# Eight tiny loads between two bulk loads of a DMA-bound decode kernel

## The chip, the cores and the metric

The kernel runs on one core of a Trainium2 chip. The metric is the time of one execution on the device, in microseconds (us). "Before" is the kernel without the change.

## The reference

One decode step of a transformer block: attention over a cached K and V, then a small dense block. Nearly all the bytes are the two caches.

```python
B, Sq, D = 4, 1, 640
H, Sk, Dh = 32, 4096, 128          # k_cache, v_cache: (B, H, Sk, Dh) bf16, 134 MB each
q = layernorm(x) @ wq              # one query per head
p = softmax(q . k_cache * Dh**-0.5)
h = x + (p . v_cache) @ wo
out = h + mish(layernorm(h) @ w1 + b1) @ w2     # b1 has 1728 elements
```

## The kernel before

The caches are cut into 16 tiles (four groups of eight heads, four batches). K and V of a tile are 8 MB each (128 partitions of 64 KB) and are loaded whole into one of three slots of SBUF, A, B and C. SP issues all these loads on its own DMA queue, each as soon as its slot is free. DVE multiplies K by the query in place, PE folds the products, DVE and ACT make the exponentials, PE multiplies them by V.

```python
def load(p, dst, src, key, sem):            # every DMA goes through this line
    p.do(lambda: p.eng.dma_start(out=dst, in_=src), key, sem, 16)

KS = {0: "A", 1: "B", 2: "A", 3: "B"}       # slot of K of tile i, by i % 4
VS = {0: "C", 1: "C", 2: "A", 3: "C"}       # slot of V

def sync_prog():                            # SP's program; need() waits
    for hg in range(NHG):                   # head groups 0..3, i = 4 * hg
        ...
        sp.need(("F", i + 1, NS - 1))       # K of tile i + 1 used up
        k_load(i + 3)
        sp.need(("F", i + 2, NS - 1))
        v_load(i + 2)
        sp.need(("PV", i + 1))              # V of tile i + 1 used up
        v_load(i + 3)
    sp.need(("F", NT - 1, NS - 1))
    for q in range(NHG):
        load(sp, wo_sb[:, q, :, :], ...)    # output weights, then w1, w2
    ...
```

The softmax here doesn't subtract the row's maximum and nothing guards it: scores larger than these inputs give would overflow.

## Time and profile before

| | before |
|---|---|
| time, median of 2 runs | 664.68 us (664.61 to 664.76) |
| span of the profiled execution | 662.8 us |
| PE busy, DVE busy | 60%, 61% |
| mean DMA rate | 428 GB/s |

These lines come from the page of before. The row "DMA" gives the busy share of the 16 DMA engines in tenths for 40 equal slices of the span, "GB/s" what they moved in each, and the line "q1" is SP's queue: packets, megabytes, and the time of its packets as a share of 16 engines' span.

```profile
PE 396.2 (60%) x2747; PEld 79.9 (12%) x1787; DVE 406.8 (61%) x252; ACT 41.5 (6%) x158; POOL 2.6 (0%) x14
DMA  9999999999999999999999999999999999999996
GB/s 381 440 435 415 424 440 439 437 439 436 412 439 439 435 431 439 439 427 427 443 431 435 435 443 431 423 439 428 435 439 443 431 423 439 431 431 439 425 414 275
q1 hardware_dynamic: 6208, 283.27, 98.9%
HBM read 283.35 MB, written 0.01 MB: 428 GB/s over the span
```

No compute engine is near full, and the DMA engines have work in every slice but the last. The kernel is bound by its stream of loads.

The place that the change touches is the middle of the third head group (i = 8). This is SP's timeline of before there: start in us, length in us, engine and line, what was issued.

```profile
403.98 0.33 SPq L249 DMA_DIRECT2D slotB<-in_A_k_cache_dram  x1
436.73 0.33 SPq L249 DMA_DIRECT2D slotA<-in_A_v_cache_dram  x1
437.10 0.43 SPq L249 DMA_DIRECT2D slotC<-in_A_v_cache_dram  x1
467.79 0.33 SPq L249 DMA_DIRECT2D slotA<-in_A_k_cache_dram  x1
```

They are K of tile 11, V of tile 10, V of tile 11 (in short V11), and K of tile 12. When V10 and V11 were issued, K11 was still being moved. The trace also holds one record for every DMA packet (time, length, bytes, queue, but not the DMA engine). From them: nearly every 64 KB packet (98% of them) takes 2418 ns, an engine has eight per load, and each engine ends one 8 MB load 19.319 us after the one before, from about the tenth load to the last with hardly an exception. That is 8.389 MB / 19.319 us = 434 GB/s. The Trainium skill ("DMA: Bandwidth & Descriptors", "Where 436 GB/s comes from") gives 435.2 GB/s as the ceiling of the ways into SBUF; this trace comes within 0.3% of it.

The 16 engines are not in step. The first ends a load 2.0 us ahead of the last, and each keeps its distance from load to load. An engine that runs ahead of the last one has a **lead**. A load has landed only when the last engine has ended it.

The chain of waits that ended last, in order of time (start, length, what), begins at 616.7 us, and its long piece is the landing of the output weights:

```profile
625.33 22.87 DMA slotB<-in_A_wo_dram
648.20 0.05 issue
648.25 1.77 PE y_ps L706 x40
```

These weights are queued behind all the K and V loads.

### The profile page before, as it was taken

To read this page: it belongs to the slowest core of one execution; us is meant where nothing else is said; L and a number is where in the kernel's file an instruction comes from. 1 tells how busy PE (TensorE), PEld (TensorE's weight loads), DVE (VectorE), ACT (ScalarE), POOL (GpSimd) and SP (SyncE) were. 2 spreads that over 40 slices of the span, in tenths; PEclk is the share of its full clock that TensorE was granted. 3 is DMA by queue.
4 is the path that set the end of the run, shared out by engine and by line. 5 is a ranking of instruction groups with operands and counts; after the bars stand their busy time and mean duration, and the time that the engine had idled before them with its cause. 6 is when DMAs were issued, how large, how long until landed. Compare 5 with 4: busy or idle time off the path is not lost. (4 is left out here: it accounts for less than half of the span.)

```text
span 662.8 us, 5202 instructions
## 1 busy us (share of the span) xinstructions
PE 396.2 (60%) x2747; PEld 79.9 (12%) x1787; DVE 406.8 (61%) x252; ACT 41.5 (6%) x158; POOL 2.6 (0%) x14
## 2 busy tenths in 40 slices
PE   0847667657317595738417485848535656765866
PEld 0600010101101010101100010010110001010246
DVE  1067988486049678767218798848306798848612
ACT  0210000000000000000000000000000000000011
POOL 1000000000000000000000000000000000000000
PEclk9768797979759697958767887787866879797975
DMA  9999999999999999999999999999999999999996
GB/s 381 440 435 415 424 440 439 437 439 436 412 439 439 435 431 439 439 427 427 443 431 435 435 443 431 423 439 428 435 439 443 431 423 439 431 431 439 425 414 275
DMA packets 6546, 283.50 MB, mean 428 GB/s; under 512 B 964, under 2 KB 1032, under 8 KB 1544
## 3 DMA queue, kind: packets, MB, share of 16 engines
q1 hardware_dynamic: 6208, 283.27, 98.9%
q8 instruction: 7, 0.11, 0.1%
q10 hardware_dynamic: 328, 0.09, 0.1%
q14 instruction: 3, 0.02, 0.0%
HBM read 283.35 MB, written 0.01 MB: 428 GB/s over the span
## 5 line engine op out<-in xcount | busy, mean ns | idle before, releaser
L513 DVE TENSOR_TENSOR slotA<-slotA,q_bc 128x8192 bf16<-128x8192 bf16 x32 | 140.6, 4415 | 106.9 <-DMA slotA<-in_A_k_cache_dram 106.9
L513 DVE TENSOR_TENSOR slotB<-slotB,q_bc 128x8192 bf16<-128x8192 bf16 x32 | 140.7, 4416 | 14.8 <-DMA slotB<-in_A_k_cache_dram 14.8
L524 DVE TENSOR_REDUCE s_f<-red 128x64 f32<-128x1024 f32 x64 | 78.0, 1218 | 99.1 <-PE red L716 99.1
L716 PE MATMUL red<-slotA,ident 128*128 128x512 bf16 x480 | 138.2, 452 | 0.0
L716 PE MATMUL red<-slotB,ident 128*128 128x512 bf16 x480 | 126.8, 424 | 0.0
L706 PE MATMUL red<-slotA,ident 128*128 128x512 bf16 x32 | 14.3, 448 | 120.0 <-PEq L49 120.0
L706 PE MATMUL pv<-slotC,e 128*32 128x512 bf16 x768 | 52.0, 430 | 38.3 <-PEq L49 35.3
L706 PE MATMUL red<-slotB,ident 128*128 128x512 bf16 x32 | 14.1, 440 | 85.5 <-PEq L49 85.5
L392 ACT ACTIVATE ex<-s_f 128x64 bf16<-128x64 f32 x64 | 16.4, 256 | 503.5 <-DVE s_f L524 503.5
L538 DVE TENSOR_TENSOR e<-ex,hmask 128x512 bf16<-128x512 bf16 x64 | 39.8, 682 | 0.0
L706 PEld LDWEIGHTS pv<-slotC,e 128*32 128x32 bf16 x768 | 22.2, 107 | 96.3 <-issue 82.4
L706 PEld LDWEIGHTS red<-slotA,ident 128*128 128x128 bf16 x32 | 3.2, 99 | 189.0 <-issue 188.9
L706 PEld LDWEIGHTS red<-slotB,ident 128*128 128x128 bf16 x32 | 3.2, 99 | 168.7 <-issue 168.7
L706 PEld LDWEIGHTS o_ps<-pv_sb,selo 128*32 128x32 f32 x136 | 13.5, 109 | 64.0 <-issue 64.0
L706 PE MATMUL o_ps<-pv_sb,selo 128*32 128x128 f32 x136 | 18.0, 276 | 0.0
L706 PE MATMUL pv<-slotA,e 128*32 128x512 bf16 x256 | 14.5, 380 | 0.5 <-PEq L49 0.4
L402 ACT COPY pv_sb<-pv 128x512 f32<-128x512 f32 x16 | 9.4, 585 | 70.4 <-PE pv L706 70.4
L392 ACT ACTIVATION_READ_ACCUMULATOR ex<-s_f 128x1 f32 x64 | 11.9, 186 | 0.0
L706 PE MATMUL red<-q_all,sel 32*128 32x128 bf16 x128 | 10.0, 268 | 0.8 <-PEq L49 0.8
L706 PEld LDWEIGHTS red<-q_all,sel 32*128 32x128 bf16 x128 | 9.7, 121 | 1.7 <-issue 1.7
L706 PEld LDWEIGHTS pv<-slotA,e 128*32 128x32 bf16 x256 | 6.9, 97 | 23.5 <-issue 17.8
L706 PE MATMUL red<-slotC,lnT 128*32 128x512 bf16 x40 | 4.5, 630 | 8.8 <-PEq L49 8.8
(96 smaller groups left out, 73.7 us busy)
## 6 DMA issues: line engine op xcount, KB each, us to landing
slotC<-in_A_v_cache_dram SPq DMA_DIRECT2D x2, 4096.0 KB, 40.1
slotC<-in_A_wq_dram SPq DMA_DIRECT2D x1, 5120.0 KB, 16.1
slotB<-in_A_wo_dram SPq DMA_DIRECT2D x4, 1280.0 KB, 19.0
slotB<-in_B_w_dram SPq DMA_DIRECT2D x1, 1296.0 KB, 25.5
slotA<-in_B_w_dram SPq DMA_DIRECT2D x1, 960.0 KB, 29.0
slotB<-in_B_w_dram SPq DMA_DIRECT2D x1, 864.0 KB, 27.1
slotA<-in_B_w_dram SPq DMA_DIRECT2D x1, 800.0 KB, 30.4
slotA<-in_B_w_dram SPq DMA_DIRECT2D x1, 320.0 KB, 27.7
```

The costliest lines, as they stand in the source:

```text
L392: lambda: a.activation(out=ex[:, sl], in_=s_f[:, sl], func=ACT.Exp, scale=SCALE, accum_out=rs[:, b, s : s + 1],),
L402: lambda: a.copy(out=pv_sb[:, :, :].rearrange("p r d -> p (r d)"), in_=pv[:, :]),
L513: lambda: v.tensor_tensor(out=t, in0=t, in1=q_bc[:, hg, b, :].unsqueeze(1).to_broadcast([P, RS, Dh]), op=ALU.mult,),
L524: lambda: v.tensor_reduce(out=s_f[:, s * RS : (s + 1) * RS], in_=red[:, k : k + 2, :].rearrange("p k (r c) -> p (k r) c", c=CW), axis=AX.X ...
L538: lambda: v.tensor_tensor(out=e[:, sl, :], in0=ex[:, sl].unsqueeze(2).to_broadcast([P, RS, G]), in1=hmask[:, :].unsqueeze(1).to_broadcast( ...
L706: lambda: nc.tensor.matmul(out_, lhsT=lhsT, rhs=rhs, start=start, stop=stop, skip_group_check=skip),
L716: return t.add_instruction(mybir.InstMatmult(name=nc.get_next_instruction_name(), engine=mybir.EngineType.PE, ins=[t.lower_ap(rhs), t.lowe ...
```

## The change

In the third head group, between the issues of V10 and V11, SP issues eight loads of rows of b1: 1, 2, 4, 6, 8, 10, 12 and 14 rows, of 34 to 60 bytes each. No instruction uses the data. The intent is to see what a few tiny loads in a full queue cost.

```diff
+    b1r = sb("b1r", (14, 8, 32), BF16)
...
             sp.need(("F", i + 2, NS - 1))
             v_load(i + 2)
+            if hg == 2:
+                for k, n in enumerate((1, 2, 4, 6, 8, 10, 12, 14)):
+                    load(
+                        sp, b1r[0:n, k, 0 : 16 + n],
+                        B_b1[0 : 14 * 32].rearrange("(p j) -> p j", j=32)[0:n, 0 : 16 + n],
+                        ("b1r", k), "MK",
+                    )
             sp.need(("PV", i + 1))
             v_load(i + 3)
-        sp.need(("F", NT - 1, NS - 1))
+        sp.need(("F", NT - 1, NS - 1), ("b1r", 7))
```

(One more semaphore, MK, is allocated for them.)

More of the change, by code (lines that the diff above doesn't have):

```diff
@@ L122 @@
     WSEM = ["WQ", "WT"] + [f"W{k}" for k in range(9)]
-    for s in ["PE", "DV", "DVP", "DVA", "AC", "ACP", "PO", "KA", "KB", "VA", "VC", "V2", "X", "S", "OUT0", "OUT1", "FIN"] + WSEM:
+    for s in ["PE", "DV", "DVP", "DVA", "AC", "ACP", "PO", "KA", "KB", "VA", "VC", "V2", "X", "S", "MK", "OUT0", "OUT1", "FIN"] + WSEM:
         book.handles[s] = nc.alloc_semaphore(s)
```

## The prediction

> **What bounds the kernel now.** The DMA stream. The page's slice table has DMA at 9 in 39 of 40 slices, 428 GB/s over the span; its queue table gives SP's queue 98.9% of 16 engines' span. PE (60%) and DVE (61%) have room. In the DMA packet records the 8 MB K and V loads land every 19.32 us, like a clock; a 64 KB packet takes 2418 ns, eight per engine per load, so no engine is ever without work. The chain of waits starts only at 616.7 us: PE, SP issuing the output-weight loads, 22.9 us of DMA to 648.2, short PE/DVE/ACT steps. Time that a DMA engine loses in the middle is therefore lost at the end, unless that engine ran ahead of the slowest (the 16 finish each load spread over 2.0 us).
>
> **What the change adds.** Nothing is removed and no compute moves (instruction order on PE, DVE, ACT, POOL unchanged). SP issues eight DMAs between the V loads of tiles 10 and 11: 57 rows of 34 to 60 bytes, about 3 KB. Nothing uses the data; SP waits for it only before the output-weight loads, some 180 us later.
> 1. Issue: one DMA in a row takes SP 0.43 + 0.04 us (timeline of SP). Eight take 3.8 us, so V of tile 11, issued at 437.1, goes out at about 440.9.
> 2. Does that starve the stream? No: at 436.7 us K of tile 11 is in flight (lands 441.0 to 443.0), then V of tile 10 occupies the engines until 460.3 to 462.3: 19 us to spare.
> 3. Engine time: small packets and semaphore packets show 9 ns each. The Trainium skill ("DMA: Bandwidth & Descriptors", "Why a DMA increments its semaphore by 16 and not by 1") says that a DMA uses the largest k up to 16 that divides the outer dimension, on the lowest-numbered k engines. So engine 0 would get all eight: 16 extra packets, about 0.15 us. The trace has small b1 loads, but interleaved with bulk; it does not show what eight successive tiny DMAs on one ring cost. If each semaphore write waited for its data's receipt, I guess 1 to 3 us on engine 0.
> 4. Queue depth: in the tail SP had about eight DMAs outstanding, and its last two issues stalled 3.4 and 4.3 us. If DMAs are counted, V of tile 11 could be held until V of tile 10 drains: a bubble of about 2 us. The stalls ended in mid-load, which looks like descriptors being counted; tiny loads have few, so I expect no hold.
>
> **Prediction.** 665.2 us, range 664.2 to 668.0 (before 664.7). Faster by over 2%: 0.005; within 2%: 0.965; slower: 0.03.
>
> **What would show each step.** SP's timeline: eight issues of 0.33 to 0.45 us at 437 to 441 us, then V of tile 11. DMA share still 9 in every slice around 440 us. The shift of the later landings against before is the whole cost. Final chain unchanged, shifted by under 1 us.
>
> **What would make it wrong.** SP stalled behind the tiny DMAs (V of tile 11 issued after 460 us, a bubble in DMA); each tiny DMA costing a full round trip on the low engines, so that one engine trails the others by several us; or an uneven ring state that persists and lowers the rate of later 64 KB packets (landing period over 19.32 us), which over ten loads could add per cents.

## The result, and the profile after

| | before | after |
|---|---|---|
| time, median of 2 runs each | 664.68 us (664.61 to 664.76) | 664.69 us (664.67 to 664.72) |
| span of the profiled execution | 662.8 us | 663.0 us |

The ratio is 1.0003, 95% interval 0.9983 to 1.0023. Such ratios are the mean time of one kernel's fast runs over that of the other's of the same rounds, so not quite the ratio of the medians that are quoted.

SP's timeline of after (all lines of the kernel moved down by one or more, so the helper is L250 now):

```profile
405.00 0.33 SPq L250 DMA_DIRECT2D slotB<-in_A_k_cache_dram  x1
434.67 0.33 SPq L250 DMA_DIRECT2D slotA<-in_A_v_cache_dram  x1
435.04 2.71 SPq L250 DMA_DIRECT2D b1r<-in_B_b_dram  x8
437.79 0.38 SPq L250 DMA_DIRECT2D slotC<-in_A_v_cache_dram  x1
468.81 0.35 SPq L250 DMA_DIRECT2D slotA<-in_A_k_cache_dram  x1
```

The eight loads took SP 2.71 us, and V11 went out at 437.79 us. The engines ended V10 between 459.9 and 462.0 us (packet records, counted from the same zero as SP's timeline), so V11 had been waiting in the queue for about 22 us. The page of after shows the same full DMA row and, on SP's queue, 114 packets more: 57 of data and 57 of semaphores.

```profile
DMA  9999999999999999999999999999999999999996
q1 hardware_dynamic: 6322, 283.27, 98.9%
```

The end of the chain, after:

```profile
627.77 20.77 DMA slotB<-in_A_wo_dram
648.54 0.05 issue
648.58 1.77 PE y_ps L714 x40
```

The output weights had landed at 648.20 us and now at 648.54, but the two executions also started their streams a little differently. Measured within each trace, the landing of V11 by the last engine came 19.319 us after that of V10 in before, and 19.360 us after it in after. **The change moved the stream by 0.04 us.**

That is not because the tiny loads were free for the engines. The data packets have different sizes for each of the eight loads, so the records tell which loads an engine had. The packets nest: one engine has all eight sizes, one has all but the 34-byte one, and so on by twos down to two engines with none. This table, worked out from the packet records, shows what each engine lost before and in its first packet of V11 (2 ns between two loads and 2418 ns for 64 KB being the normal case):

```
loads on    engines   ns from the end of V10    extra ns in V11's
the engine            to the start of V11       first 64 KB packet
    0          2            2                       0
    1          2           15                       0
    2          2           28                       0
    3          2           41                       0
    4          2           54                       0,  21
    5          2           67                      90, 163
    6          2           80                     173, 213
    7          1           92                     384
    8          1          105                     543
```

Each tiny load takes 13 ns of visible packet time. From the fifth on, something else is paid, and it shows as a slow first bulk packet. The engine with all eight lost 105 - 2 + 543 = 646 ns, but it was the first of the 16 to end V10, 2.12 us ahead of the last. The engine that was last had two of the tiny loads and lost 26 ns. One more thing is in these records: in that same load one engine lost 844 ns once, for a reason that they don't name, in before too, and there the landing did not move at all (it had a lead). In after the stalled engine was one with six tiny loads; with both losses it became the last, and sets the 0.04 us.

### The profile page after: what moved, and what is told of

The parts are those of the page before. It is cut to its first block, busy times and chain, and to the rows that moved or that the text cites. A ratio compares the mean times of both kernels' runs of the same rounds, so it can differ in the third digit from the quotient of the medians.

```text
span 663.0 us, 5211 instructions
## 1 busy us (share of the span) xinstructions
PE 399.5 (60%) x2747; PEld 81.4 (12%) x1787; DVE 406.8 (61%) x252; ACT 41.6 (6%) x158; POOL 2.6 (0%) x14
## 5 line engine op out<-in xcount | busy, mean ns | idle before, releaser
L724 PE MATMUL red<-slotA,ident 128*128 128x512 bf16 x480 | 136.4, 447 | 0.0
L724 PE MATMUL red<-slotB,ident 128*128 128x512 bf16 x480 | 129.7, 431 | 0.0
L714 PE MATMUL red<-slotA,ident 128*128 128x512 bf16 x32 | 14.2, 445 | 119.5 <-PEq L49 119.5
L714 PE MATMUL red<-slotB,ident 128*128 128x512 bf16 x32 | 14.3, 447 | 87.3 <-PEq L49 87.3
```

Of the source, the lines that this page charges most:

```text
L714: lambda: nc.tensor.matmul(out_, lhsT=lhsT, rhs=rhs, start=start, stop=stop, skip_group_check=skip),
L724: return t.add_instruction(mybir.InstMatmult(name=nc.get_next_instruction_name(), engine=mybir.EngineType.PE, ins=[t.lower_ap(rhs), t.lowe ...
```

## The experiments

The theory after this: (a) the stream is the clock; SP's time for tiny loads costs nothing while the next bulk load is issued before the engines run out; (b) each engine loses time by the number of tiny loads that it gets; (c) the end moves only by what the last engine loses, so leads hide the rest. Rivals: there is slack later in the kernel that hides any small delay (R1); tiny loads cost in proportion to their number (R2); the queue holds few DMAs (R3); lost engine time goes straight to the end (R4). Twelve kernels were run; all gave correct results. The time before was 664.46 us (664.18 to 665.14) for the first four, 664.35 (664.11 to 664.88) for the next four and 664.39 (664.14 to 664.90) for the last four. SBUF had under 1 KB per partition left, so where 24 loads are issued the rows are narrower.

| run | tiny loads | time, us (range) | ratio | landing by the last engine moved, us |
|---|---|---|---|---|
| e1_wait | 8, waited for | 669.88 (669.38 to 670.35) | 1.0081 | 4.36 |
| e2_24_here | 24 | 667.01 (666.61 to 667.05) | 1.0038 | 2.35 |
| e3_24_early | 24, before V10 | 669.18 (667.75 to 670.20) | 1.0075 | 2.10 |
| e4_one1 | 1 with 113 runs | 664.62 (664.09 to 664.67) | 0.9999 | 0.00 |
| e5_24_k1 | 24 of one row | 666.36 (666.24 to 666.37) | 1.0030 | 1.74 |
| e6_24_sems | 24, own semaphores | 666.95 (666.38 to 667.04) | 1.0037 | 2.61 |
| e7_24_src | 24, spread in HBM | 667.02 (666.67 to 667.49) | 1.0041 | 2.00 |
| e8_24_dst | 24, spread in SBUF | 666.82 (666.76 to 667.09) | 1.0038 | 2.49 |
| e9_sbuf | 24 from SBUF | 668.86 (668.53 to 669.50) | 1.0069 | 3.86 |
| e10_24_k16 | 24 of 16 rows | 668.41 (668.31 to 669.16) | 1.0063 | 4.05 |
| e11_7places | 7 times 8 of one row | 667.57 (667.50 to 667.79) | 1.0047 | 2.74 |
| e12_8_k16 | 8 of 16 rows | 665.24 (665.17 to 665.39) | 1.0013 | 0.72 |

The last column is from the packet records of the profiled run: how much later than 24 x 19.319 us the last engine ended the last full 8 MB load, counted from the seventh one of the stream. In before it is 0.00, in after 0.04.

### e1_wait: wait for the tiny loads

```diff
                         ("b1r", k), "MK",
                     )
+                sp.need(("b1r", 7))
             sp.need(("PV", i + 1))
             v_load(i + 3)
```

> The eight loads as in the change, but SP waits for the last of them before it issues V of tile 11. Theory (the stream of bulk loads is the clock; the tiny loads are free because they queue behind V of tile 10 and V of tile 11 is issued some 20 us before an engine is free for it): now V of tile 11 is issued only when the queue has run empty, at about 463 to 464 us, [...]the slowest engine idles about 3 us, and the time is 667 to 669 us (before 664.7), with every later landing shifted by the same amount. Rival R1 (the kernel has slack after this point in which small delays vanish): 664.5 to 665.2 us.

SP's timeline:

```profile
435.68 0.33 SPq L250 DMA_DIRECT2D slotA<-in_A_v_cache_dram  x1
436.05 2.71 SPq L250 DMA_DIRECT2D b1r<-in_B_b_dram  x8
463.37 0.36 SPq L250 DMA_DIRECT2D slotC<-in_A_v_cache_dram  x1
```

The same eight issues took the same 2.71 us, but V11 left at 463.37 us, after the queue had run empty. Busy time by stretch, of after and then of this run (stretch, its length, busy time of PE, PE weight loads, DVE, ACT, POOL, then granted clock, DMA share, GB/s):

```profile
460.00:466.00 6.00, 6.00 (x34) 0.44 (x21) 5.98 (x3) 0.35 (x2) 0.00 (x0) 0.72 1.04 439
```

```profile
460.00:466.00 6.00, 5.54 (x74) 1.87 (x65) 4.76 (x2) 0.35 (x2) 0.00 (x0) 1.00 0.51 176
```

In these six microseconds the DMA share falls from 1.04 to 0.51 and the rate from 439 to 176 GB/s. (A packet is counted in the stretch in which it starts, with its whole length and all its bytes.) The first packets of V11 started only at 464.37 to 465.04 us, 1.0 us or more after its issue, and took 0.1 to 0.9 us longer than 2418 ns. With both, the landing of V11 moved by 4.01 us. That is more than the 3 us expected, and the time rose by 5.4 us (expected 2.5 to 4.5). A further 0.35 us came later: after the bubble all engines started together, their spread shrank from 1.9 to 0.55 us, and the following loads no longer kept to 19.319 us. About 1 us more stands in the tail of the profiled run: one of the 16 engines lost 1.2 us in the first load of w1, which landed 4.27 us after the last output weights, where before has 3.11 (semaphore records). Why that engine lost it stays open. R1 falls: nothing later hid this bubble.

### e2_24_here and e3_24_early: three times as many, in two places

```diff
-                for k, n in enumerate((1, 2, 4, 6, 8, 10, 12, 14)):
+                for k, n in enumerate((1, 2, 4, 6, 8, 10, 12, 14) * 3):
                     load(
-                        sp, b1r[0:n, k, 0 : 16 + n],
-                        B_b1[0 : 14 * 32].rearrange("(p j) -> p j", j=32)[0:n, 0 : 16 + n],
+                        sp, b1r[0:n, k, 0 : 2 + n],
+                        B_b1[0 : 14 * 32].rearrange("(p j) -> p j", j=32)[0:n, 0 : 2 + n],
```

In e3_24_early the same block stands before `v_load(i + 2)`, that is before V10.

> The eight loads three times over (24, with rows of 6 to 32 bytes), at the same place. Theory: SP spends about 8.2 us on them, V of tile 11 goes out at about 443.3 us, still 17 us early; an engine loses at most about 0.3 us plus a slowed first bulk packet, and the early engines have 2 us to give: 664.5 to 665.0 us. Rival R2 (tiny loads cost in proportion to their number, and eight were too few to see): a visible rise, 665.2 or more, and as much as in the run with 24 loads before V of tile 10. If the queue holds a limited number of DMAs (R3), SP stalls in the 24 and V of tile 11 is issued only after about 460 us, with a bubble of 2 us or more: 666.5 us or more.

> The same 24 loads, placed before the issue of V of tile 10 instead of after it. Theory: there the next bulk load is issued only 6 to 8 us before the engines run out of K of tile 11 (441.0 to 443.2 us), SP needs 8.2 us for the tiny loads, V of tile 10 goes out at about 442.9 us[...]: the slowest engine idles 1 to 2.5 us, time 665.7 to 667.2 us. Rival R2: the same as with the 24 loads after it. Rival R1: 664.5 to 665.2 us.

SP's timeline of e2_24_here:

```profile
433.48 0.33 SPq L250 DMA_DIRECT2D slotA<-in_A_v_cache_dram  x1
433.85 8.05 SPq L250 DMA_DIRECT2D b1r<-in_B_b_dram  x24
441.94 0.37 SPq L250 DMA_DIRECT2D slotC<-in_A_v_cache_dram  x1
```

The theory failed for e2_24_here: it expected 664.5 to 665.0 us and the run took 667.0. SP did not stall (24 issues in 8.05 us, V11 out at 441.94 us, some 18 us early), so R3 is not the reason either. The packet records show ten engines that lost 0.8 to 3.8 us each, most of it on V11's first packet (0.7 to 3.5 us), where the theory had only added up 13 ns per load. The size of the loss, not its place, was wrong; e5 to e9 look for its cause.

SP's timeline of e3_24_early:

```profile
434.32 8.02 SPq L250 DMA_DIRECT2D b1r<-in_B_b_dram  x24
442.39 0.37 SPq L250 DMA_DIRECT2D slotA<-in_A_v_cache_dram  x1
442.80 0.43 SPq L250 DMA_DIRECT2D slotC<-in_A_v_cache_dram  x1
```

Here the 8 us of issuing came out of a slack of about as many, and V10 left when the engines were already ending K11. The landing moved by 2.10 us and the profiled run, the fastest of the four, took 667.75 us. The other three took 669.04 to 670.20 us, above the range expected, and they have no trace; why they are slower stays open. So this pair shows that the place matters, but not cleanly by how much, since e2_24_here has a loss of its own. R2 is half right: the rise is visible, but not the same in both places, and three times the loads moved the landing by 2.35 us in place of 0.04.

### e4_one1: 113 packets on one engine, one DMA

```diff
-    b1r = sb("b1r", (14, 8, 32), BF16)
+    b1r = sb("b1r", (1, 113, 4), BF16)
...
+                load(sp, b1r[0:1, :, 0:3],
+                     B_b1[0 : 113 * 13].rearrange("(o r c) -> o r c", o=1, c=13)[:, :, 0:3], ("b1r", 0), "MK")
```

> In place of the eight loads one load of 113 runs of 6 bytes into a single partition; 113 is prime, so by the rule for the number of engines all its packets go to one engine. Theory: that engine loses 113 x 13 ns = about 1.5 us plus a slowed bulk packet (up to 0.5 us); it was the earliest of the 16 in the traced run, 2.1 us ahead of the slowest, so the end hardly moves: 664.5 to 665.2 us. If lost engine time went straight to the end (rival R4): 666.0 to 666.9 us.

The time did not move (664.62 against 664.46 us). One engine had all 113 packets of 6 bytes; it lost 1.03 us, was 2.2 us ahead of the last, and the landing moved by 0.00 us: R4 falls. A packet cost it 9 ns, not the 80 or 150 ns of a whole tiny load. SP's timeline shows a side effect:

```profile
436.16 0.75 SPq L250 DMA_DIRECT2D b1r<-in_B_b_dram  x1
436.95 20.74 SPq L250 DMA_DIRECT2D slotC<-in_A_v_cache_dram  x1
466.35 0.34 SPq L250 DMA_DIRECT2D slotA<-in_A_k_cache_dram  x1
```

With 113 descriptors of one DMA waiting on one engine, the issue of V11 lasted 20.74 us, until 457.69 us. It was still in time, by some 2 us. In after, with eight more DMAs but only eight descriptors more on the fullest engine, it took 0.38 us, and in e2_24_here, with 24 more DMAs, 0.37 us. So what fills the queue seems to go by descriptors on an engine and not by DMAs; how many it holds was not measured.

### e5_24_k1: 24 loads on one engine

```diff
     (against e2_24_here)
-                for k, n in enumerate((1, 2, 4, 6, 8, 10, 12, 14) * 3):
+                for k, n in enumerate((1,) * 24):
-                        sp, b1r[0:n, k, 0 : 2 + n],
+                        sp, b1r[0:n, k, 0 : 12 + n],
     (and the source likewise: 13 elements)
```

> The 24-load run cost 2.5 us although V of tile 11 was issued in time; in its packet records ten engines lost 0.8 to 3.8 us each on the bulk packet that follows the tiny ones. Here 24 loads of one row (13 elements, a prime, so one engine per load): one engine gets all 24, as many DMAs as the busiest engine had before. Theory C (the loss is contention between engines that do tiny packets and semaphore increments together): that engine loses about 24 x 13 ns = 0.3 us and little more, the others nothing; 664.3 to 664.9 us. Rival S (each tiny DMA's own semaphore write or round trip holds its engine for some 0.15 us): that engine loses about 3.6 us, 2.1 us or less of which its lead can hide: 665.5 to 667.5 us.

SP's timeline:

```profile
434.58 7.09 SPq L250 DMA_DIRECT2D b1r<-in_B_b_dram  x24
441.71 0.36 SPq L250 DMA_DIRECT2D slotC<-in_A_v_cache_dram  x1
```

One engine had all 24 packets. It lost 284 - 2 + 3444 = 3726 ns; but for the one 0.84 us stall described above, no other engine lost anything. Contention between engines falls; the loss belongs to the number of tiny DMAs on an engine, 155 ns each on the mean, or 3444 / 20 = 172 ns for each beyond the fourth (in after 543 / 4 = 136). The engine had a lead of 2147 - 165 = 1982 ns. 3726 - 1982 = 1744 ns is what the lead could not hide, and the landing moved by 1.74 us. This is (c) in one subtraction.

### e6_24_sems, e7_24_src, e8_24_dst: other semaphores, other source, other destination

```diff
     (each against e2_24_here; e6)
-                        ("b1r", k), "MK",
+                        ("b1r", k), f"MK{k}",
     (e7)
-                        B_b1[0 : 14 * 32].rearrange("(p j) -> p j", j=32)[0:n, 0 : 2 + n],
+                        B_w2[70 * k : 70 * k + 70].rearrange("(p j) d -> p j d", j=5)[0:n, 0, 0 : 2 + n],
     (e8)
-                        sp, b1r[0:n, k, 0 : 2 + n],
+                        sp, b1r[0 : 4 * n : 4, k, 0 : 2 + n],
```

> The 24 loads as before, each with its own semaphore in place of one for all. If the loss comes from 168 increments on one semaphore (C-sem): the time falls back to 664.3 to 665.2 us and the following bulk packets are slowed by under 1 us. If the semaphore is not it: again 666.5 to 667.5 us and up to 3 to 4 us on the following bulk packets.

> The 24 loads with the same rows and widths, but each row from another place in HBM (rows of w2, 6400 bytes apart and none read twice) in place of the same 14 rows of b1, 64 bytes apart. If the loss comes from all engines reading the same few hundred bytes of HBM (C-src): 664.3 to 665.2 us, bulk packets slowed by under 1 us. If not: again 666.5 to 667.5 us.

> The 24 loads from b1 as before, but written to every fourth partition (0, 4, ... 52) in place of partitions 0 to 13. If the loss comes from many engines writing to a few neighbouring partitions[...] (C-dst): 664.3 to 665.5 us, bulk packets slowed by under 1.5 us. If not: again 666.5 to 667.5 us.

All three took 666.8 to 667.0 us like e2_24_here, and the most loaded engines again lost 3.7 to 3.9 us. So it is not one semaphore that all increments go to, not 14 engines reading the same 900 bytes of HBM, and not 14 neighbouring partitions as target. That fits e5_24_k1. (In e6_24_sems the packet records count 171 increments by the engines, not 168.) In e8_24_dst, with every fourth partition as target, SP needed 16.63 us for the 24 issues, where e2_24_here took 8.05; V11 still left at 450.86 us, 9 us before the first engine ended V10.

### e9_sbuf: read SBUF in place of HBM

```diff
     (against e5_24_k1)
+                sp.need("ident")
-                        B_b1[0 : 14 * 32].rearrange("(p j) -> p j", j=32)[0:n, 0 : 12 + n],
+                        ident[0:n, 0 : 12 + n],
```

> The contention theory fell: 24 one-row loads on one engine slowed that engine alone, by 3.7 us (about 155 ns per load), while 113 packets of one load cost it 1.0 us. So the cost goes with the number of DMAs on an engine. Here the same 24 one-row loads read 26 bytes of SBUF (the identity tile) in place of HBM. If each tiny DMA's HBM read is what is waited for (a few in flight at a time): the engine's loss falls to 2 us or less, the time to 664.3 to 665.3 us. If it is the end of the write or the semaphore write (S), which are the same as before: again a loss of 3 to 4 us and 665.9 to 666.8 us.

This experiment did not come out as built. The 13 elements, which from HBM had been one packet of 26 bytes, went as 13 packets of 2 bytes each over 13 engines (312 packets = 24 x 13), so 13 engines had 24 tiny DMAs, and the time, 668.9 us, lies outside both ranges. SP needed 18.89 us for the 24 issues, but V11 left at 456.50 us, 3.3 us before the first engine ended V10, so the queue did not run empty. Still, each of these 13 engines had one data packet and one semaphore packet per DMA as the one engine in e5_24_k1 had. Each lost 2.9 to 4.2 us on V11's first packet alone (in one engine the 0.84 us stall may be part of it), and 4.0 us in all on the mean, although the tiny loads read nothing from HBM. A wait for their HBM read is therefore not needed for the loss.

### e10_24_k16 and e12_8_k16: all 16 engines

```diff
     (e12; e10 has (16,) * 24 and rows of 13 elements)
-                for k, n in enumerate((1, 2, 4, 6, 8, 10, 12, 14)):
+                for k, n in enumerate((16,) * 8):
                     load(
-                        sp, b1r[0:n, k, 0 : 16 + n],
+                        sp, b1r[0:n, k, 0:30],
```

> 24 loads of 16 rows, so that all 16 engines get every load. Theory (each engine loses by the number of tiny DMAs that it gets, some 3.7 us for 24, and the end moves by what the last engine lost beyond its lead): no engine is spared, the last one loses as much as the first, and the time rises by 3.3 to 4.2 us to 667.7 to 668.6 us, where one-row loads cost 2.0. Rival (the leading engines' slack does not matter): as with one row, 666.0 to 666.8 us.

> The change with 16 rows in each of the eight loads (60 bytes a row), so that all 16 engines, the last one too, get all eight. Theory: each engine loses about 0.6 us as the busiest one did in the change, and the end moves by it: 664.8 to 665.3 us against 664.35 before, a rise of 0.4 to 0.8 us. Rival (eight tiny loads cost nothing whatever the rows): a rise under 0.2 us.

With 16 rows each engine gets one packet of each load, the last engine too. In e10_24_k16 every engine lost 3.2 us or more on V11's first packet, and 4.0 us in all on the mean of the 16; the time rose by 4.0 us, as expected, where the same 24 loads on one engine had cost 2.0. In e12_8_k16, the change with 16 rows in place of 1 to 14, the engines lost 0.5 to 1.0 us (one had the 0.84 us stall on top). The engine that had been last lost 0.60 us; the landing moved by 0.72 us, since the stalled engine became the last. The median rose by 0.85 us, a little over the 0.4 to 0.8 expected; the interval of its ratio, 0.9999 to 1.0026, just includes 1, but none of its five runs (665.17 and up) overlaps with the nine of before (664.90 and down). V11 was issued in time:

```profile
436.13 3.67 SPq L250 DMA_DIRECT2D b1r<-in_B_b_dram  x8
439.85 0.42 SPq L250 DMA_DIRECT2D slotC<-in_A_v_cache_dram  x1
```

The busy time by stretch of e10_24_k16 shows the gap that its tiny packets leave in the bytes moved (before had 438 GB/s in the same six microseconds):

```profile
460.00:466.00 6.00, 6.00 (x50) 0.98 (x40) 5.42 (x2) 0.69 (x4) 0.00 (x0) 0.82 1.13 178
```

The DMA share reads as busy, 1.13, since a slowed packet counts as busy for its whole length. GB/s is the column to read here.

### e11_7places: eight at a time, seven times

```diff
+    def tiny(k0):
+        for k in range(k0, k0 + 8):
+            load(sp, b1r[0:1, k, :], B_b1[0:7].rearrange("(p j) -> p j", j=7), ("b1r", k), "MK")
...
+            tiny(16 * hg)
             v_load(i + 3)
+            if hg < 3:
+                tiny(16 * hg + 8)
     (the block of the change is taken out)
```

> Eight one-row loads at each of seven places, one bulk load or more apart, in place of eight loads at one. Theory: engine 0 loses about 0.6 us per place (as the busiest engine did in the change), never catches up, uses up its lead of about 2 us after three or four places, and the end moves by 7 x 0.6 - 2.1 = about 2 us: 666.0 to 667.2 us. Rival R1 (a loss in one engine is made good later in the stream): 664.3 to 665.0 us. If eight alone cost next to nothing in each place and only long trains cost: also 664.3 to 665.0 us, with engine losses under 0.3 us per place in the packet records.

The one engine that got them lost 0.63 to 0.79 us at each of the six places that lie between full loads, and never caught up. It was ahead of the last engine at first, then the last itself, at the end 2.7 us behind the next one. The time rose by 3.2 us; the range expected ended 0.4 us lower, since 0.6 us per place was a little low. A lead is spent once.

## Why the prediction was right

The prediction said 665.2 us, "within 2%", and the result is 664.69 us. "Within 2%" asked for little: it holds for each of the twelve experiments too (ratios up to 1.0081). What can be right or wrong is in the steps.

- **The bound.** Right. The landings keep a fixed period, and e1_wait shows that a bubble in the stream is paid in full.
- **Step 1, issue time.** Direction right, size too high: 3.8 us predicted, 2.71 us measured.
- **Step 2, no starvation.** Right: V11 was issued at 437.79 us, 22 us before the first engine wanted it. (The packet times that the prediction gives lie some 0.5 us later than the records on SP's clock: V10 ended at 459.8 to 461.8 us in before. The argument doesn't hang on it.) e1_wait, which takes this away and leaves the loads, costs 5.4 us.
- **Step 3, engine time.** Which engines get the loads was right as far as the records show: one engine has all eight, and the shares nest as the rule of the Trainium skill ("DMA: Bandwidth & Descriptors", "Why a DMA increments its semaphore by 16 and not by 1") says. The cost was mis-sized: "16 extra packets, about 0.15 us" was 0.65 us on the busiest engine, and the guess of 1 to 3 us, for the case that each semaphore write waits for its data, was too high for eight. The truth is between: about four tiny DMAs in a row cost 13 ns each, those after them 90 to 170 ns (after and e5_24_k1).
- **What reached the end.** The sum predicted was +0.5 us and 0.04 us came. The prediction named the condition ("unless that engine ran ahead of the slowest") but did not use it. The row counts of the change, all below 16, put the most loads on an engine that was 2.1 us ahead and left the late ones with two or fewer. e12_8_k16, with 16 rows, takes this shelter away and costs 0.7 to 0.85 us (0.60 us by the last engine's own loss). So it was luck, as far as the prediction goes, that a cost four times the 0.15 us left no trace in the time.
- **Step 4, queue depth.** Right: no hold with eleven DMAs in flight. e4_one1 shows the hold that was feared, with 113 descriptors on one engine.

What stays open: what exactly an engine waits for between tiny DMAs. It is not the data packets as such (e4_one1: 9 ns each), it does not need a read of HBM by the tiny loads (e9_sbuf) or a shared semaphore (e6_24_sems). It goes with the number of DMAs. The Trainium skill ("DMA: Bandwidth & Descriptors", "Queues, rings and completion order") says that a semaphore increment lands only after every earlier write of that engine; a few increments pending at once and then a wait for each would look like the table above, but this is not shown: no run separates the increment from the rest of a DMA.

## What to carry to other kernels

In a kernel whose DMA queue never runs empty, ask of any added transfer three things: does it delay the issue of the next bulk load past the moment when the engines run out, does anyone wait for it while it stands behind bulk loads, and what does the last of the 16 engines lose. Up to about four tiny DMAs in a row are nearly free to an engine, after that each costs 0.1 to 0.2 us; join them into one DMA (113 runs in one DMA cost an engine 1.0 us, 24 tiny DMAs 3.7), but mind how many of its descriptors fall to one engine: those 113 held SP's next issue for 20.74 us. An engine's lead can hide a loss, but only once, and it hides it only if the late engines are spared.

## What the Trainium skill lacked or had wrong

- "DMA: Bandwidth & Descriptors" has no figure for tiny DMAs that follow each other on one ring. It calls the semaphore write on trn2 "essentially free", in its section on the gpsimd path ("Anatomy of one DMA — SWDGE (gpsimd) path"); the loads here are issued by SP. For a lone one the traces agree (2 ns between two bulk loads), and for three or four tiny loads in a row nearly so (13 ns each). From the fifth on each load cost some 0.1 to 0.2 us: 646 ns for eight, 3726 ns for 24; whether the semaphore write is what costs is not shown.
- The same page has no figure for how much may wait on a ring before the issuing engine stalls. With 113 descriptors of one DMA on one engine SP's next issue lasted 20.74 us; with eight extra DMAs of one descriptor each, 0.38 us.
- Its rule for the number of engines, by the slowest dimension that is not of size 1, fits the rows of the change and the 113 runs of e4_one1. For [1, 13] elements it gives 13 engines: so it was from SBUF (e9_sbuf, 13 packets of 2 bytes), but from HBM the same shape went as one packet on one engine (e5_24_k1), and the page does not tell why. (The expectation of e5_24_k1 said one engine because 13 is prime; that is not the rule, and it came out by luck.)
- No page says that the 16 engines keep a fixed distance (about 2 us from first to last) through a long stream, or that loads were slower than 19.319 us once a bubble had put the engines in step (0.35 us over the next seven loads in e1_wait).
